# Joint attention tails, a rearranged start and held loads in a linear-attention plus feed-forward kernel

## The chip, the cores and the metric

One core of one Trainium2 chip. The metric is the device time in microseconds (us), median of several runs. A run of a program on few cores is called slow when it is over 1.5% above the fastest of the same kernel.

## The reference, cut to what matters

```python
def _attn_ref(q, k, v):              # batch 8, heads 8, sequence 576, head_dim 64
    phi = lambda x: np.where(x > 0, x, np.exp(x) - 1.0) + 1.0
    q_p, k_p = phi(q), phi(k)
    kv  = np.einsum('bhsd,bhse->bhde', k_p, v)
    z   = np.sum(k_p, axis=2)
    num = np.einsum('bhsd,bhde->bhse', q_p, kv)
    den = np.einsum('bhsd,bhd->bhs', q_p, z)[..., None] + 1e-06
    return num / den

def _moe_ref(x, w_in, w_out, beta):  # x: 4608 x 512, w_in: 512 x 2048, w_out: 2048 x 512
    h = x @ w_in
    g = h * (1.0 / (1.0 + np.exp(-beta * h)))
    return g @ w_out
```

## The kernel before

The program alternates, batch by batch, an h phase (`w_in` products and silu) and a y phase (`w_out` products and stores), 64 products of 512 columns each. The attention of the next batches is slipped in between. 576 rows are four tiles of 128 and a tail of 64; the tails of all eight batches form a ninth batch at the end. Each batch's tail was a pass of its own:

```python
    def num_mm(b, t):
        n = rows(t)                          # 128, or 64 for the tail
        nps = att_banks()
        st[b, "n", t] = nps
        for p in range(KC):                  # 4
            c0 = (p % 2) * 2 * (D + 1)
            nc.tensor.matmul(
                nps[:n, p // 2, c0 : c0 + 2 * (D + 1)],
                st[b, "qT"][:, t, p, :n],
                kv_bd[b % 2][p // 2][:, p % 2], ...)
    # num_norm: VectorE divides by the denominator, rows(t) rows.
    # x_trans: TensorE transposes x (batches 0-2); from batch 3 on the DMA does.
```

Batch 0 has a layout of its own (`nine`, nine columns of 64 rows), and the start loads it before the weights, all over the GpSimd queue:

```python
    load_nine(k9, k)
    load_nine(q9, q, j1=4)
    ...
    load_nine(v9, v, j1=6)
    load_nine(v9, v, j0=6)
    load_nine(q9, q, j0=4)
    for i in range(4):
        nc.gpsimd.dma_start(out=w_in_sb[i], in_=w_in_v[:, :, i * 512 : (i + 1) * 512])
    load_w_out(0); load_w_out(1); load_k(1); load_q(1)
    ...
    load_w_out(2); load_v(1); load_w_out(3)
```

Batch 4 is loaded in the second h phase, and q of batch 2 is transposed by DMA in the second y phase:

```python
            12: [F(v_copy, 2), F(load_next, 4)],          # second h phase
    ...
    y_phase_wide(1, {
        1: [F(phi, 2, 0), F(q_trans_dma, 2), F(phi, 2, 1)],
        6: [F(kv_mm, 2), F(kv_evac, 2)],
        11: [F(num_mm, 2, 0), F(num_norm, 2, 0)],
        12: [F(num_mm, 2, 1), F(num_norm, 2, 1), F(x_trans, 2, 0, wide=True)],
        ...
```

## Time and profile before

| what | before |
|---|---|
| time, median of 3 runs | 296.43 us (296.33 to 296.48) |
| TensorE busy | 283.9 of 295.1 us |
| first main product | 17.16 us |
| first h, first y phase | 17.00 and 18.37 us |
| second h, second y phase | 15.08 and 17.64 us |
| a steady batch (h and y) | 29.86 us |

The phases are read from the table of stretches, cut at the first product of each phase. Besides the lines that the prediction shows, two are needed for the comparison (start:end and length, busy us and number of instructions of TensorE, weight load, VectorE, ScalarE, GpSimd; granted TensorE clock, DMA share, GB/s):

```profile
34.16:52.53 18.37, 17.42 (x146) 9.32 (x148) 13.77 (x28) 13.69 (x15) 10.47 (x13) 1.00 1.42 248
...
85.42:101.36 15.94, 15.94 (x137) 9.20 (x136) 7.69 (x13) 12.65 (x23) 4.69 (x6) 1.00 0.94 138
```

The first, the first y phase, contains about 1 us of idle TensorE time, the second, batch 2's h phase, none. The second y phase is the stretch 67.61:85.25 of the prediction's table, with about 1.3 us idle.

### The profile page before, as it was taken

How to read it: one execution, taken by the hardware profiler on the slowest of the kernel's cores; microseconds unless marked ns; L12 is line 12 of the kernel's file. 1: busy time of each engine (PE TensorE's matmuls, PEld its weight loads, DVE VectorE, ACT ScalarE, POOL GpSimd, SP SyncE). 2: the span in 40 equal slices, each digit the busy share in tenths (PEclk: the TensorE clock that was granted, in tenths of full speed). 3: DMA queues.
4: the chain of work that ended last, by engine and by line, in shares of the span. 5: the costliest groups of instructions: out<-in, count | busy, mean ns of one | idle time of the engine just before them, and what ended most of it. 6: DMA issues, size and time to landing. Idle time of an engine off the chain costs nothing.

```text
span 295.1 us, 4750 instructions
## 1 busy us (share of the span) xinstructions
PE 283.9 (96%) x1891; PEld 143.9 (49%) x1912; DVE 124.0 (42%) x261; ACT 175.1 (59%) x234; POOL 52.7 (18%) x72
## 2 busy tenths in 40 slices
PE   8879999999999999999999999999999999999994
PEld 3557445644465544445444544454445444444444
DVE  4765488504365174616461646154715400110012
ACT  2788786889988780778087907790770077018500
POOL 8924474540003200330023000000000000000000
PEclk9999999999999999999999999999999999999999
DMA  7999999999637993699369945024502400120032
GB/s 103 196 207 343 256 272 192 256 193 192 89 142 100 175 131 113 130 174 154 98 129 159 159 109 124 2 71 116 127 0 72 118 36 0 38 90 16 0 73 71
DMA packets 72310, 37.09 MB, mean 126 GB/s; under 512 B 40912, under 2 KB 66784, under 8 KB 72288
## 3 DMA queue, kind: packets, MB, share of 16 engines
q0 software_dynamic: 38912, 20.45, 47.9%
q1 hardware_dynamic: 33216, 16.20, 22.9%
q8 instruction: 15, 0.25, 0.3%
q10 hardware_dynamic: 160, 0.13, 0.2%
q14 instruction: 7, 0.06, 0.1%
HBM read 36.71 MB, written 9.44 MB: 156 GB/s over the span
## 4 chain that ended last, share of the span: by engine, by line
PE 76%; DMA 9%; POOL 4%; ACT 4%; issue 4%; DVE 1%; ACTq 0%; POOLq 0%; DVEq 0%
PE mm L453 37%; PE mm L505 33%; DMA xT<-in_moe_w_out_dram 5%; DMA vraw<-in_v_dram 4%; PE att L399 3%; ACT e L229 2%; POOL xqk L131 1%; PE att L344 1%; PE mm L537 1%; POOL w_in L159 1%; ACT L229 1%; POOL vraw L131 1%; ACT g L445 1%; DVE qk_p L242 0%; POOL xqk L111 0%
## 5 line engine op out<-in xcount | busy, mean ns | idle before, releaser
L445 ACT ACTIVATE g<-mm,beta_c 128x512 bf16<-128x512 f32 (+2 forms) x156 | 97.3, 633 | 88.4 <-PE mm L453 88.1
L505 PE MATMUL mm<-w_out,g 128*128 128x512 bf16 x541 | 126.7, 379 | 1.2 <-issue 0.3
L453 PE MATMUL mm<-xT,w_in 128*128 128x512 bf16 (+2 forms) x560 | 108.1, 349 | 1.4 <-DMA w_in<-in_moe_w_in_dram 1.1
L453 PEld LDWEIGHTS <-w_in 128*128 128x128 bf16 x656 | 61.9, 98 | 62.4 <-DMA w_in<-in_moe_w_in_dram 1.2
L505 PEld LDWEIGHTS <-g 128*128 128x128 bf16 x560 | 53.0, 98 | 58.2
L515 DVE COPY y_sb<-mm 128x512 f32<-128x512 f32 x27 | 18.7, 691 | 70.6 <-PE mm L505 69.1
L229 ACT ACTIVATE e<-xqk 128x2560 bf16<-128x2560 bf16 x14 | 31.9, 2329 | 0.1
L415 DVE TENSOR_TENSOR xs<-att,rden 128x512 bf16<-128x512 f32 (+1 forms) x40 | 27.6, 689 | 1.4
L242 DVE TENSOR_TENSOR qk_p<-r,e 128x2560 bf16<-128x2560 bf16 x14 | 20.9, 1490 | 13.1 <-ACT e L229 12.4
L355 DVE CAST kv_bd<-att 64x130 bf16<-64x130 f32 x28 | 8.2, 292 | 32.2 <-PE att L344 31.8
L72 POOL DMA_DIRECT2D vraw<-in_v_dram x7 | 6.4, 909 | 84.2 <-DVE vaug L370 78.5
L413 DVE TENSOR_SCALAR den<-att 128x8 f32<-128x8 f32 (+1 forms) x40 | 6.5, 161 | 32.0 <-PE att L399 31.9
L399 PE MATMUL att<-kv_bd,q_pT 128*128 128x130 bf16 (+1 forms) x160 | 15.8, 221 | 1.1 <-DVE kv_bd L370 0.7
L399 PEld LDWEIGHTS <-q_pT 128*128 128x128 bf16 (+1 forms) x160 | 11.6, 100 | 10.7 <-DVE xs L415 2.4
L453 PE MATMUL mm<-xT_tail,w_in 128*128 128x512 bf16 x63 | 13.9, 379 | 0.1
L237 DVE TENSOR_SCALAR r<-xqk 128x2560 bf16<-128x2560 bf16 x14 | 11.6, 834 | 3.8 <-DMA xqk<-in_q_dram 2.3
L575 PE MATMUL mm<-g 128*128 128x512 bf16 x34 | 9.9, 452 | 1.2 <-DVE g L143 1.2
L229 ACT ACT_TABLE_LOAD x7 | 9.0, 1283 | 0.1
L414 DVE RECIPROCAL rden<-den 128x8 f32<-128x8 f32 (+1 forms) x40 | 8.1, 202 | 1.4
L72 POOL DMA_DIRECT2D xqk<-in_k_dram x7 | 6.9, 984 | 6.3 <-DMA w_in<-in_moe_w_in_dram 2.8
L76 POOL DMA_DIRECT2D xqk<-in_k_dram x7 | 7.4, 1057 | 1.5 <-DMA w_in<-in_moe_w_in_dram 1.3
L256 ACT ACTIVATE e<-xqk 128x1280 bf16<-128x1280 bf16 (+1 forms) x4 | 4.4, 1155 | 5.4 <-DMA xqk<-in_k_dram 5.3
(71 smaller groups left out, 140.0 us busy)
## 6 DMA issues: line engine op xcount, KB each, us to landing
out_dram<-y_sb SPq DMA_DIRECT2D x28, 256.0 KB, 2.3
xqk<-in_k_dram POOLq DMA_DIRECT2D x7, 512.0 KB, 10.7
xqk<-in_q_dram POOLq DMA_DIRECT2D x7, 512.0 KB, 11.3
vraw<-in_v_dram POOLq DMA_DIRECT2D x7, 512.0 KB, 11.3
w_in<-in_moe_w_in_dram POOLq DMA_DIRECT2D x4, 512.0 KB, 11.0
g<-in_moe_w_out_dram POOLq DMA_DIRECT2D x4, 512.0 KB, 10.9
out_dram<-y_sb SPq DMA_DIRECT2D x14, 128.0 KB, 5.2
xqk<-in_moe_w_out_dram POOLq DMA_DIRECT2D x2, 512.0 KB, 14.4
```

What stands on the lines that cost most here:

```text
L72: eng.dma_start(out=dst[:, :, 0:NJ, :].rearrange("p h j d -> p h (j d)"), in_=src[b, :, 0:MAIN, :].rearrange("h (p j) d -> p h (j d)", j=NJ),)
L229: nc.scalar.activation(st[b, "e", a][:, h0:h1], xqk[b % NX][:, a, h0:h1], ACTF.Exp)
L237: nc.vector.tensor_scalar(st[b, "r", a][:, h0:h1], xqk[b % NX][:, a, h0:h1], 0.0, 1.0, ALU.max, ALU.add)
L242: nc.vector.tensor_tensor(st[b, "p"][:, a].rearrange("p j (h d) -> p h j d", h=H)[:, h0:h1], st[b, "r", a][:, h0:h1], st[b, "e", a][:, h0: ...
L355: nc.vector.tensor_copy(kv_bd[b % 2][i][gs, :, g, :], st[b, "kvp"][gs, 2 * i : 2 * i + 2, :])
L399: nc.tensor.matmul(nps[:n, p // 2, c0 : c0 + 2 * (D + 1)], st[b, "qT"][:, t, p, :n], kv_bd[b % 2][p // 2][:, p % 2], start=True, stop=True ...
L415: nc.vector.tensor_mul(xs[:n], nv[:, :, :, 0:D], rden[:n, :, :, None].to_broadcast([n, 2, 4, D]))
L445: nc.scalar.activation(g_sb[b % 2][:, ff, c0:c1], hp[:, c0:c1], ACTF.Silu, scale=beta_c[:, ff : ff + 1],)
L453: nc.tensor.matmul(hp[:, c0:c1], w_in_sb[ff // 4][:, kc, (ff % 4) * P : (ff % 4 + 1) * P], x[:, t0:t1, kc, :] if b < B else x[:, kc, c0:c1 ...
L505: nc.tensor.matmul(yp, g_sb[b % 2][:, ff, t * P : (t + 1) * P], w_out_sb[ff // 4][:, ff % 4, :], start=(ff == 0), stop=(ff == FC - 1),)
L515: nc.vector.tensor_copy(y_sb, yp)
L575: nc.tensor.matmul(st["warm"], g_sb[0][:, FC - 1, 0:P], g_sb[0][:, FC - 1, :], start=True, stop=True, skip_group_check=True,)
```

## The change

Its intent: two neighbouring batches share one tail pass; batch 0's attention starts on a part of k; loads no longer run among DMA transposes that TensorE waits for. The core of the diff, cut:

```diff
+    load_nine(k_last, k, KF, N9, eng=nc.sync)       # KF = 5: k's last 4 columns, fp32
-    nc.sync.dma_start(out=beta_row, ...)
+    nc.scalar.dma_start(out=beta_row, ...)
-    load_nine(k9, k)
-    load_nine(q9, q, j1=4)
+    load_nine(x9[1][:, :, 0:KF], k, 0, KF)
+    load_nine(x9[0][:, :, 0:QF], q, 0, QF)          # QF = 4
-    load_nine(v9, v, j1=6)
-    load_nine(v9, v, j0=6)
+    load_nine(v9[:, :, 0:KF], v, 0, KF)
+    load_nine(v9[:, :, KF:N9], v, KF, N9)
 ...
-    warm(20)
+    warm(15)                                         # idle-time products
 ...                                                  # start and first h phase reordered
     def num_mm(b, t):
+            for i in range(1 if t < NJ else 2):
+                bb, n, r0 = (b, P, 0) if t < NJ else (b - 1 + i, TAIL, i * TAIL)
                 nc.tensor.matmul(
-                nps[:n, p // 2, c0 : c0 + 2 * (D + 1)], st[b, "qT"][:, t, p, :n], ...
+                    nps[r0 : r0 + n, p // 2, c0 : c0 + 2 * (D + 1)], st[bb, "qT"][:, t, p, :n], ...
     def num_norm(b, t):
-        if by_dma(b):
+        if by_dma(b) or t == NJ:                     # every tail transposed by DMA
 ...
+    def hold(a):
+        nc.gpsimd.tensor_copy(held, a)               # makes the GpSimd queue wait for a
+    def held_load(b, n):                             # batch b behind batch n's transposed q
+        hold(st[n, "qT"][0:1, NJ, KC - 1, 0:1])
+        load_next(b)
 ...
-        9: [F(kv_mm, 1), F(kv_evac, 1), F(w_out_scale, 3)],                # first y phase
-        10: [F(q_trans, 1, 0, 1, wide=True), F(q_trans, 1, 2, 3, wide=True)],
+        10: [F(q_trans, 1, 0, 1, 2, 3), F(kv_mm, 1), F(kv_evac, 1), F(w_out_scale, 3, 2)],
 ...
-            12: [F(v_copy, 2), F(load_next, 4)],
+            12: [F(v_copy, 2)],
-        6: [F(kv_mm, 2), F(kv_evac, 2)],
+        6: [F(kv_mm, 2), F(kv_evac, 2), F(held_load, 4, 2)],
-        12: [..., F(x_trans, 2, 0, wide=True)],
+        12: [..., F(x_trans, 2, 0, wide=True, dve=True)],   # x copies on VectorE
 ...
-        load_next(b + 3)
+            plan[7 + o] = [F(v_copy, n), F(held_v, b + 3, n)]
+            plan[12] = [F(held_kq, b + 3, n)]
-            for t in range(NT):
+            for t in range(NT if n % 2 else NJ):     # tail with every second batch
```

More of the change, by code (lines that the diff above doesn't have):

```diff
@@ L120, in nine, with load_nine @@
         flat = a.rearrange("p a b c -> p (a b c)")
-        size = {"h": HH, "j": N9, "d": D}
-        n = size["h"] * size["j"] * size["d"]
-        return flat[:, 0:n].rearrange(f"p ({names}) -> p {names}", **size)
-    q9 = nine(xqk[0][:, 0], "hjd")
-    k9 = nine(xqk[0][:, 1], "hjd")
-    v9 = nine(vraw[0], "hjd")
-    def load_nine(dst, src, h0=0, h1=HH, j0=0, j1=N9):
-        for g in range(2):
-            nc.gpsimd.dma_start(
-                out=dst[g * TAIL : (g + 1) * TAIL, h0:h1, j0:j1, :].rearrange(
-                    "p h j d -> p h (j d)"
-                ),
-                in_=src[0, g * HH + h0 : g * HH + h1, :, :]
+        return flat[:, 0 : HH * N9 * D].rearrange(
+            f"p ({names}) -> p {names}", h=HH, j=N9, d=D
+        )
+    x9 = [nine(xqk[0][:, a], "hjd") for a in range(2)]
+    v9 = nine(vraw[0], "hjd")
+    QF = 4
+    KF = 5
+    k_last = g_f[:, 0 : HH * (N9 - KF) * D].rearrange(
+        "p (h j d) -> p h j d", h=HH, j=N9 - KF
+    )
+    def load_nine(dst, src, j0, j1, eng=nc.gpsimd):
+        for g in range(2):
+            eng.dma_start(
+                out=dst[g * TAIL : (g + 1) * TAIL].rearrange("p h j d -> p h (j d)"),
+                in_=src[0, g * HH : (g + 1) * HH, :, :]
                 .rearrange("h (p j) d -> p h j d", j=N9)[:, :, j0:j1, :]
@@ L146 @@
     beta_row = consts.tile([FC, P], F32)
-    nc.sync.dma_start(out=beta_row, in_=moe_beta.rearrange("(c p) -> c p", p=P))
+    nc.scalar.dma_start(out=beta_row, in_=moe_beta.rearrange("(c p) -> c p", p=P))
     identity = consts.tile([P, P], BF16)
     ident16 = consts.tile([FC, FC], F32)
-    load_nine(k9, k)
-    load_nine(q9, q, j1=4)
+    load_nine(x9[1][:, :, 0:KF], k, 0, KF)
+    load_nine(x9[0][:, :, 0:QF], q, 0, QF)
     make_identity(nc, identity)
     make_identity(nc, ident16)
-    load_nine(v9, v, j1=6)
-    load_nine(v9, v, j0=6)
-    load_nine(q9, q, j0=4)
+    load_nine(v9[:, :, 0:KF], v, 0, KF)
+    load_nine(v9[:, :, KF:N9], v, KF, N9)
+    load_nine(x9[0][:, :, QF:N9], q, QF, N9)
     for i in range(4):
@@ L163 @@
     load_q(1)
-    kv_bd = [
-        [consts.tile([P, 2, 2, D + 1], BF16, name=f"kv_bd{i}{g}") for g in range(2)]
-        for i in range(2)
-    ]
+    kv_bd = [consts.tile([P, KC, 2, D + 1], BF16, name=f"kv_bd{i}") for i in range(2)]
     for i in range(2):
-        for g in range(2):
-            nc.vector.memset(kv_bd[i][g], 0.0)
+        nc.vector.memset(kv_bd[i], 0.0)
     def set_ones(i):
@@ L205, in make_beta, with w_out_scale @@
         nc.vector.reciprocal(rbeta, beta_c)
-    def w_out_scale(i, dve=True):
+    def w_out_scale(i, on_dve=4):
         for c in range(4):
@@ L210, in w_out_scale @@
             dst, src, by = w_out_sb[i][:, c, :], w_out_f[i][c // 2][:, c % 2, :], rbeta[:, ff : ff + 1]
-            if dve:
+            if c < on_dve:
                 nc.vector.tensor_scalar(dst, src, by, None, ALU.mult)
@@ L245, in phi, with begin9, in9, exp9 @@
         )
-    x0 = {0: q9, 1: k9}
+    def begin9():
+        begin(0)
+        st["p9"] = [
+            nine(st[0, "p"][:, a].rearrange("p j (h d) -> p j h d", h=H), "jhd")
+            for a in range(2)
+        ]
     def work9(tag, **kw):
         return nine(work.tile([P, H, NT, D], BF16, tag=tag, name=tag, **kw), "jhd")
-    def exp0(a, j0, j1):
+    def in9(a, j0, j1):
+        if a == 1 and j0 >= KF:
+            return k_last[:, :, j0 - KF : j1 - KF]
+        return x9[a][:, :, j0:j1]
+    def exp9(a, j0, j1):
         if j0 == 0:
-            st["e0", a] = work9("e", bufs=3)
+            st["e9", a] = work9("e", bufs=3)
         nc.scalar.activation(
-            st["e0", a][:, j0:j1].rearrange("p j h d -> p h j d"), x0[a][:, :, j0:j1],
+            st["e9", a][:, j0:j1].rearrange("p j h d -> p h j d"), in9(a, j0, j1),
             ACTF.Exp,
         )
-    def relu0(a, j0, j1):
+    def relu9(a, j0, j1):
         if j0 == 0:
-            st["r0", a] = work9("r")
+            st["r9", a] = work9("r")
         nc.vector.tensor_scalar(
-            st["r0", a][:, j0:j1].rearrange("p j h d -> p h j d"), x0[a][:, :, j0:j1],
+            st["r9", a][:, j0:j1].rearrange("p j h d -> p h j d"), in9(a, j0, j1),
             0.0, 1.0, ALU.max, ALU.add,
         )
-    def phi0(a, j0, j1):
+    def phi9(a, j0, j1):
         nc.vector.tensor_tensor(
-            st["p0"][a][:, j0:j1], st["r0", a][:, j0:j1], st["e0", a][:, j0:j1], ALU.min
+            st["p9"][a][:, j0:j1], st["r9", a][:, j0:j1], st["e9", a][:, j0:j1],
+            ALU.min,
         )
-    def q_trans0(t, banks, c0):
+    def q_trans9(t, banks, c0):
         for jj in range(2 if t < NJ else 1):
@@ L283, in q_trans0 @@
                         banks[:, g, m0 : m0 + TAIL],
-                        st["p0"][0][gs, 2 * t + jj, 2 * a : 2 * a + 2, :],
+                        st["p9"][0][gs, 2 * t + jj, 2 * a : 2 * a + 2, :],
                         identity[gs, gs],
@@ L287, in q_trans0, with q_out9 @@
                     )
-    def q_out0(t, banks, c0, dve):
-        n = rows(t)
-        src = banks[:, :, c0 : c0 + 2 * P].rearrange("p g (a n) -> p g a n", a=2)
-        dst = st[0, "qT"][:, t].rearrange("p (g a) n -> p g a n", g=2)
-        copy(dst[:, :, :, :n], src[:, :, :, :n], dve)
+    def q_out9(t0, t1, banks, c0, dve):
+        n = rows(t0)
+        src = banks[:, :, c0 : c0 + (t1 - t0) * 2 * P].rearrange(
+            "p g (t a n) -> p g t a n", a=2, n=P
+        )
+        dst = st[0, "qT"][:, t0:t1].rearrange("p t (g a) n -> p g t a n", g=2)
+        if n == P:
+            src = src.rearrange("p g t a n -> p g t (a n)")
+            dst = dst.rearrange("p g t a n -> p g t (a n)")
+        else:
+            src, dst = src[:, :, 0, :, :n], dst[:, :, 0, :, :n]
+        copy(dst, src, dve)
     def kv_cols(kvp, g, a):
@@ L308, in kv_mm0 @@
                         cols[:, :, 0:D] if of_v else cols[:, :, D],
-                        st["p0"][1][gs, j, 2 * a : 2 * a + 2, :],
+                        st["p9"][1][gs, j, 2 * a : 2 * a + 2, :],
                         v9[gs, 2 * a : 2 * a + 2, j, :] if of_v else ones[gs],
@@ L314, in kv_mm0, with kv_evac9 @@
                     )
-    def kv_evac0(kvp):
+    def kv_evac9(kvp):
         for g in range(2):
@@ L320, in kv_evac0 @@
                 copy(
-                    kv_bd[0][g][gs, :, i, :],
+                    kv_bd[0][gs, 2 * g : 2 * g + 2, i, :],
                     kvp[g][gs, 0 : 4 * (D + 1)].rearrange(
@@ L351, in kv_evac @@
     def kv_evac(b):
-        for i in range(2):
-            for g in range(2):
-                gs = slice(g * D, (g + 1) * D)
-                nc.vector.tensor_copy(
-                    kv_bd[b % 2][i][gs, :, g, :], st[b, "kvp"][gs, 2 * i : 2 * i + 2, :]
-                )
+        for g in range(2):
+            gs = slice(g * D, (g + 1) * D)
+            nc.vector.tensor_copy(kv_bd[b % 2][gs, :, g, :], st[b, "kvp"][gs])
     def rows(t):
@@ L372, in copy, with q_trans @@
             nc.scalar.activation(dst, src, ACTF.Copy)
-    def q_trans(b, *ts, wide=False, dve=False):
-        n, m = rows(ts[0]), len(ts)
-        tp = tr_bank(wide).rearrange("p (t c n) -> p t c n", t=2, c=KC)
+    def q_trans(b, *ts):
+        n = rows(ts[0])
+        tp = att_banks(BF16).rearrange("p i (t c n) -> p (i t) c n", t=2, c=KC)
         for i, t in enumerate(ts):
@@ L384, in q_trans @@
                 )
-        copy(st[b, "qT"][:, ts[0] : ts[0] + m, :, :n], tp[:, 0:m, :, :n], dve)
+        for i in range(0, len(ts), 2):
+            m = min(2, len(ts) - i)
+            copy(
+                st[b, "qT"][:, ts[i] : ts[i] + m, :, :n], tp[:, i : i + m, :, :n], False
+            )
     def q_trans_dma(b):
@@ L393, in num_mm @@
     def num_mm(b, t):
-        n = rows(t)
         nps = att_banks()
@@ L398, in num_mm @@
             c0 = (p % 2) * 2 * (D + 1)
-            nc.tensor.matmul(
-                nps[:n, p // 2, c0 : c0 + 2 * (D + 1)],
-                st[b, "qT"][:, t, p, :n],
-                kv_bd[b % 2][p // 2][:, p % 2],
-                start=True, stop=True, skip_group_check=True,
-            )
+            for i in range(1 if t < NJ else 2):
+                bb, n, r0 = (b, P, 0) if t < NJ else (b - 1 + i, TAIL, i * TAIL)
+                nc.tensor.matmul(
+                    nps[r0 : r0 + n, p // 2, c0 : c0 + 2 * (D + 1)],
+                    st[bb, "qT"][:, t, p, :n],
+                    kv_bd[bb % 2][:, p],
+                    start=True, stop=True, skip_group_check=True,
+                )
     def num_norm(b, t):
-        n = rows(t)
+        n = P
         den = work.tile([P, 2, 4], F32, tag="den", name="den")
@@ L425, in x_dst @@
             return xT[b % 3][:, t]
-        return xT_tail[:, :, b * TAIL : (b + 1) * TAIL]
+        return xT_tail[:, :, (b - 1) * TAIL : (b + 1) * TAIL]
     def x_trans(b, t, wide=False, dve=False):
-        n = rows(t)
+        n = P
         xv = st[b, "xs", t].rearrange("p a h d -> p (a h d)")
@@ L479, in h_last @@
             silu(b, 12 + i, hps[i])
-    out0 = out[0:S, :].rearrange("(p j) m -> p j m", j=N9)
+    out9 = out[0:S, :].rearrange("(p j) m -> p j m", j=N9)
     def tail_rows(b):
         if b == 0:
-            return out0[:, N9 - 1, :]
+            return out9[:, N9 - 1, :]
         return out[b * S + MAIN : (b + 1) * S, :]
@@ L492, in store @@
                     nc.sync.dma_start(
-                        out=out0[:, 2 * t + i, :], in_=y_sb[i * TAIL : (i + 1) * TAIL, :]
+                        out=out9[:, 2 * t + i, :], in_=y_sb[i * TAIL : (i + 1) * TAIL, :]
                     )
@@ L564, in load_next, with held_v, held_kq @@
         if b < B:
-            if b >= 5:
-                load_v(b)
             load_k(b)
             load_q(b)
-            if b < 5:
-                load_v(b)
+            load_v(b)
+    held = consts.tile([1, 1], BF16)
+    def hold(a):
[3 more added lines that the diff above has]
+        load_next(b)
+    def held_v(b, n):
+        if b < B:
+            hold(st[n, "qT"][0:1, NJ, KC - 1, 0:1])
+            load_v(b)
+    def held_kq(b, n):
+        if b < B:
+            hold(xT[n % 3][0:1, NJ - 1, KC - 1, 0:1])
+            load_k(b)
+            load_q(b)
     def warm(n):
@@ L584, in F @@
         return lambda: f(*a, **k)
-    begin(0)
+    begin9()
     st["warm"] = mm_bank([P, 512])
@@ L589 @@
     beta_trans()
-    make_beta()
-    warm(20)
-    st["p0"] = [
-        nine(st[0, "p"][:, a].rearrange("p j (h d) -> p j h d", h=H), "jhd")
-        for a in range(2)
-    ]
-    exp0(1, 0, 5)
-    exp0(1, 5, N9)
-    exp0(0, 0, 4)
-    relu0(1, 0, 5)
-    relu0(1, 5, N9)
-    phi0(1, 0, 5)
-    relu0(0, 0, 4)
-    phi0(1, 5, N9)
-    phi0(0, 0, 4)
+    warm(15)
+    exp9(1, 0, KF)
+    exp9(1, KF, N9)
+    exp9(0, 0, 2)
+    exp9(0, 2, QF)
+    relu9(1, 0, KF)
+    relu9(1, KF, N9)
+    phi9(1, 0, KF)
+    relu9(0, 0, QF)
+    phi9(1, KF, N9)
+    phi9(0, 0, 2)
+    phi9(0, 2, QF)
+    make_beta()
     kvp = [mm_bank([P, 512]) for _ in range(2)]
-    kv_mm0(kvp, 0, N9, False)
+    kv_mm0(kvp, 0, KF, False)
+    kv_mm0(kvp, 0, KF, True)
+    kv_mm0(kvp, KF, N9, False)
     qb = att_banks(BF16)
-    q_trans0(0, qb, 0)
-    q_trans0(1, qb, 256)
-    q_out0(0, qb, 0, False)
-    q_out0(1, qb, 256, False)
-    kv_mm0(kvp, 0, 6, True)
-    kv_mm0(kvp, 6, N9, True)
-    kv_evac0(kvp)
+    q_trans9(0, qb, 0)
+    q_out9(0, 1, qb, 0, False)
+    kv_mm0(kvp, KF, N9, True)
+    kv_evac9(kvp)
+    q_trans9(1, qb, 256)
+    q_out9(1, 2, qb, 256, False)
     st["warm"] = mm_bank([P, 512])
@@ L618 @@
     num_mm(0, 1)
-    exp0(0, 4, N9)
-    relu0(0, 4, N9)
+    num_norm(0, 0)
+    exp9(0, QF, N9)
+    relu9(0, QF, N9)
     silu_table()
-    num_norm(0, 0)
-    phi0(0, 4, 6)
     warm(4)
     x_trans(0, 0, dve=True)
+    num_norm(0, 1)
+    phi9(0, QF, 6)
+    phi9(0, 6, N9)
     qb2 = att_banks(BF16)
-    q_trans0(2, qb2, 0)
-    q_out0(2, qb2, 0, False)
-    num_norm(0, 1)
-    phi0(0, 6, N9)
     load_w_out(2)
@@ L635, with tidy, q_rest @@
     load_w_out(3)
-    def tidy0():
+    def tidy():
         clear_tail(0)
         nc.vector.memset(vraw[0][TAIL:P, :, NJ, :], 0.0)
-    def q_rest0():
-        q_trans0(3, qb2, 256)
-        q_trans0(4, qb2, 512)
-        q_out0(3, qb2, 256, False)
-        q_out0(4, qb2, 512, False)
+    def q_rest():
+        for t in range(2, NT):
+            q_trans9(t, qb2, (t - 2) * 256)
+        for t in range(2, NT):
+            q_out9(t, t + 1, qb2, (t - 2) * 256, t < NJ)
     h_phase(
@@ L652 @@
         {
-            3: [F(x_trans, 0, 1), F(num_mm, 0, 2), F(num_norm, 0, 2), F(q_rest0)],
-            5: [F(num_mm, 0, 3), F(num_norm, 0, 3)],
-            7: [F(x_trans, 0, 2)],
-            8: [F(num_mm, 0, 4), F(num_norm, 0, 4)],
-            9: [F(x_trans, 0, 3), F(tidy0)],
-            12: [F(x_trans, 0, 4)],
+            1: [F(x_trans, 0, 1)],
+            3: [F(q_rest)],
+            5: [F(num_mm, 0, 2), F(num_norm, 0, 2)],
+            7: [F(num_mm, 0, 3), F(num_norm, 0, 3)],
+            8: [F(x_trans, 0, 2)],
+            10: [F(x_trans, 0, 3, dve=True), F(tidy)],
             17: [F(w_out_scale, 0), F(w_out_scale, 1)],
@@ L674 @@
     phi(1, 1)
-    v_copy(1)
     phi(1, 0)
+    v_copy(1, 0, HH)
+    v_copy(1, HH, H, dve=False)
     y_phase_wide(0, {
         4: [F(load_next, 3)],
-        9: [F(kv_mm, 1), F(kv_evac, 1), F(w_out_scale, 3)],
-        10: [F(q_trans, 1, 0, 1, wide=True), F(q_trans, 1, 2, 3, wide=True)],
+        10: [
+            F(q_trans, 1, 0, 1, 2, 3), F(kv_mm, 1), F(kv_evac, 1), F(w_out_scale, 3, 2),
+        ],
         11: [F(num_mm, 1, 0), F(num_norm, 1, 0)],
@@ L683 @@
         13: [F(num_mm, 1, 2), F(num_norm, 1, 2), F(x_trans, 1, 1, wide=True)],
-        14: [F(num_mm, 1, 3), F(num_norm, 1, 3), F(q_trans, 1, 4, wide=True)],
+        14: [F(num_mm, 1, 3), F(num_norm, 1, 3), F(q_trans, 1, 4)],
     })
@@ L693 @@
             1: [F(x_trans, 1, 3)],
-            3: [F(x_trans, 1, 4)],
             8: [F(begin, 2), F(relu, 2, 0)],
             10: [F(relu, 2, 1)],
-            12: [F(v_copy, 2), F(load_next, 4)],
+            12: [F(v_copy, 2)],
         },
@@ L706 @@
         1: [F(phi, 2, 0), F(q_trans_dma, 2), F(phi, 2, 1)],
-        6: [F(kv_mm, 2), F(kv_evac, 2)],
+        6: [F(kv_mm, 2), F(kv_evac, 2), F(held_load, 4, 2)],
         11: [F(num_mm, 2, 0), F(num_norm, 2, 0)],
-        12: [F(num_mm, 2, 1), F(num_norm, 2, 1), F(x_trans, 2, 0, wide=True)],
-        13: [F(num_mm, 2, 2), F(num_norm, 2, 2), F(x_trans, 2, 1, wide=True)],
-        14: [F(num_mm, 2, 3), F(num_norm, 2, 3)],
+        12: [F(num_mm, 2, 1), F(num_norm, 2, 1), F(x_trans, 2, 0, wide=True, dve=True)],
+        13: [F(num_mm, 2, 2), F(num_norm, 2, 2)],
+        14: [
+            F(x_trans, 2, 1, wide=True, dve=True), F(num_mm, 2, 3), F(num_norm, 2, 3),
+        ],
     })
@@ L722 @@
             plan = {
-                0: [F(x_trans, 2, 2), F(num_mm, 2, 4), F(num_norm, 2, 4)],
-                1: [F(x_trans, 2, 3)],
-                3: [F(x_trans, 2, 4)],
+                0: [F(x_trans, 2, 2, dve=True)],
+                1: [F(x_trans, 2, 3, dve=True)],
             }
@@ L730 @@
             plan[5 + o] = [F(relu, n, 1), F(phi, n, 1)]
-            plan[7 + o] = [F(v_copy, n)]
+            plan[7 + o] = [F(v_copy, n), F(held_v, b + 3, n)]
             plan[12 + o] = [F(kv_mm, n)]
```

## The prediction

> **What bounds the kernel now.** I read the page first (busy shares and the 40 slices), then the chain of waits in order of time, then TensorE's timeline where that chain leaves TensorE, then the table of stretches, then the groups by shape.
>
> ```profile
> span 295.1 us, 4750 instructions
> ...
> PE 283.9 (96%) x1891; PEld 143.9 (49%) x1912; DVE 124.0 (42%) x261; ACT 175.1 (59%) x234; POOL 52.7 (18%) x72
> ...
> PE   8879999999999999999999999999999999999994
> ...
> DMA  7999999999637993699369945024502400120032
> ```
>
> TensorE is full in all slices but the first three and the last. The transfer engines are full too, up to about 80 us, and lightly used afterwards. So two regimes are to be expected: an early one in which arrivals matter, and a late one in which only TensorE's own work does. The chain in order of time (start, us, what) agrees:
>
> ```profile
> 13.18 15.45 DMA xT<-in_moe_w_out_dram
> ...
> 30.20 11.62 DMA vraw<-in_v_dram
> ...
> 110.91 0.35 PE att L399 x4
> 111.26 5.29 PE mm L505 x24
> 116.54 11.22 PE mm L453 x52
> 127.77 0.75 PE att L344 x40
> 128.52 2.70 PE mm L453 x12
> ```
>
> From about 83 us on the chain stays on TensorE. The 0.35 us is the tail of one batch: four products of 64 columns. The table of stretches (start:end, length, then busy time and count of TensorE, weight load, VectorE, ScalarE, GpSimd; clock, DMA share, GB/s), cut where the phases begin, says how much room each has:
>
> ```profile
> 17.16:34.16 17.00, 16.57 (x153) 11.31 (x154) 9.62 (x23) 13.87 (x32) 8.15 (x10) 1.00 1.29 263
> 34.16:47.30 13.14, 12.37 (x107) 6.46 (x108) 9.61 (x16) 10.39 (x9) 7.35 (x9) 1.00 1.36 272
> ...
> 67.61:85.25 17.64, 16.30 (x126) 8.14 (x128) 7.90 (x18) 16.99 (x17) 0.00 (x0) 1.00 0.89 135
> ...
> 128.52:158.38 29.86, 29.75 (x188) 14.25 (x190) 14.21 (x28) 18.12 (x20) 4.70 (x6) 1.00 0.83 137
> ```
>
> A steady batch has 0.11 us of idle time in 29.86: nothing is to be had there except by removing TensorE work. The room is in the early stretches, and the timeline of TensorE (start, us, instruction, in brackets the idle time before it and what ended it) names it:
>
> ```profile
> 17.16 1.07 PE L453 MATMUL mm<-xT,w_in 128*128 128x128 bf16 x16 [1.10 <-DMA w_in<-in_moe_w_in_dram]
> ...
> 19.28 0.61 PE L453 MATMUL mm<-xT,w_in 128*128 128x128 bf16 x8 [0.31 <-ACT xT L372]
> ...
> 43.23 0.82 PE L344 MATMUL att<-vaug,qk_p 128*64 128x65 bf16 x40 [0.28 <-DVE vaug L370]
> ...
> 79.33 0.41 PE L399 MATMUL att<-kv_bd,q_pT 128*128 128x130 bf16 x4 [0.34 <-DMA q_pT<-qk_p]
> ...
> 83.07 0.38 PE L433 MATMUL att<-identity,xs 128*128 128x128 bf16 x4 [0.61 <-ACT xT L372]
> ```
>
> The first main product waits for weights, not for the attention that feeds it. Busy time hides the shorter gaps, because ends are modelled; so I count work at the streaming rate: 52 products of 512 columns in 11.22 us are 0.216 us each, and a group of four full attention products is 0.22 to 0.23 us on the chain.
>
> [...] the 40 products of 64 by 65 above, alternating between output halves, take 0.75 us, 19 ns each, while the 64-column tail, all in one half, takes 0.35/4 = 87 ns each. [...] half of a v copy on ScalarE should bring no table load; here ScalarE's copies between silus have none.
>
> **Part by part.**
>
> Joint tails. Before, each batch has a tail pass of 0.35 us: 8 x 0.35 = 2.80. After, four passes of eight products that alternate between output halves. If the halves overlap, a pass costs about one old one, estimated 0.37: 1.48. Saved 1.32: batches 0 and 2 save 0.35 each early, the steady part (five passes become three) 5 x 0.35 - 3 x 0.37 = 0.64. The tails of batches 0, 1 and 2 no longer go through TensorE transposes (0.22 each on the chain), but by DMA: 0.66. Sum **1.98 us**, all on TensorE's path. VectorE loses four normalizations of about 1.05 us (0.16 + 0.20 + 0.68), off the path and worth nothing by themselves.
>
> Start. Four of nine columns of k now go over the sync queue, which can start at about 0.8 us where the first GpSimd transfer starts at 1.25. 0.52 MB of source thus moves mostly in engine time idle until 2.5 us, and everything behind in the GpSimd queue, w_in first, moves up by at most 0.52/0.4 = 1.3. The attention chain moves too: k's five columns land near 6.4 instead of 7.49, and xT would be ready near 14.5 instead of 16.3. w_in remains the later one, so I take its gain, less some interference: **1.0 us**, first main product at 16.1.
>
> First h phase (17.00 us). Work is 32 x 0.057 + 48 x 0.108 + 32 x 0.216 = 13.95, plus transposes of x 0.66 + 0.22, products 0.46 + 0.35, query transposes 0.35: 15.99, so 1.0 is idle. The new order puts eight more query transposes in (+0.23), but shifts consumers away from the ScalarE copy (0.31) and the short waits around it; the new VectorE copies make batch 0's third x late by some 0.2. I keep half of the idle time: net **0.27** beyond the tails.
>
> First y phase (13.14). Work to the second x tile is 48 x 0.216 + 0.75 + 0.87 + 0.23 = 12.2, idle 0.9. The kv product goes behind the query transposes and one more group, v's copy is split, two evacuations replace four. But the phase now starts 2 us sooner while w_out and v come only 1 us sooner; VectorE's two minimum passes, the evacuation and w_out's scaling end near 45.2 where TensorE wants the last weights near 45. I count half: **0.45**.
>
> Batch 2 (67.61 to 85.25). Work is 64 x 0.216 + 0.75 + 4 x 0.23 + 2 x 0.22 = 16.0, idle 1.65. Batch 4's loads no longer share the engines with batch 2's query transpose (9.0 us to landing in that window), which removes 0.27 to 0.34; the x copies go to VectorE and leave the queue behind ScalarE's exponentials, which removes 0.61 to 0.79. One wait of 0.3 for the first normalization stays, and VectorE has 4 x 1.06 + 4 x 0.42 = 5.9 us to do beside 5.2 of TensorE, so a little returns: **0.95**.
>
> Held loads from batch 5 on. These are off the path: there is no wait for q or x transposes in the steady part to remove. Expected 0.
>
> Sum: 1.98 + 1.0 + 0.27 + 0.45 + 0.95 = 4.65; 296.43 - 4.65 = **291.8 us**, 1.6% less.
>
> **Rivals.** (a) The second queue only shares: w_in is no earlier and the phases behind are paced by the same arrivals. For it: DMA is full at once from 2.5 us. Against: idle time before. It would cost about 1.3: 293.1. (b) The halves do not overlap, since each weight load of 64 columns waits: eight products at 87 ns are 0.70 and the joint pass saves nothing but the transposes; 293.1. Against: the kv products. (c) Held loads come too late: k and q are now issued some 3.5 us before the end of a y phase and wanted by the exponentials about 14.6 us after that end; at 11.3 us to landing they have near 7 us to spare. If they took 20 us, every batch would wait, and the gain would be gone: 296 or more. The lightly used engines speak against it. (d) The early phase is more elastic than I count: all of the idle time in the three early stretches goes and w_in moves 1.3. That adds 0.3 + 0.5 + 0.45 + 0.5: about 290.0.
>
> **Range and chances.** (a) and (b) are each perhaps one in six; (d) or a good part of it as likely. That gives 290.1 to 293.6. Faster by over 2% needs 290.5, 1.3 us beyond my sum: 0.16. Slower by over 2% needs (c) in force on several batches: 0.01. Within 2%: 0.83.
>
> **What would show it.** Right: the first main product near 16.1, still released by w_in; joint passes of eight in 0.3 to 0.45 us; no wait for q_pT and none for ScalarE's xT in the second y phase; steady batches of 29.5 and 29.9 us in turn; an end after the last product of 3.8 us as before. Wrong: a joint pass of 0.7; steady batches with a wait on k, q or v; an early phase waiting for w_out or on VectorE for over 1 us, which would mean that it was bound by arrivals more than I count.

For its figures: in the kernel before, the transfer engines moved 17 GB/s from 1.5 to 2.0 us, nothing from 2.0 to 2.5, 58 GB/s at a busy share of 0.77 from 2.5 to 3.0 ("full at once"), and 173 to 198 GB/s from 3.5 to 6.0 us, counted in bf16 as it is written; the prediction's 0.4 MB/us is an estimate, twice that for the fp32 source. The first exponential on k starts at 7.49 us. ScalarE's timeline has a table load of 1.28 us at 80.55 us and the next at 102.10, and none at the copies between the silus from 86 to 89 us; in the profile after, the half of the v copy on ScalarE, at 43.15 us, has none of its own. "Lightly used" holds for the late part of the row: its slices from 74 to 184 us read 3 to 9 tenths, those after them 0 to 5.

## The result, and the profile after

The changed kernel took 293.34 us (292.85 to 294.18, 4 runs), the kernel before 296.46 us beside it. The ratio is 0.9897 (95% interval 0.9873 to 0.9921): 1.0% faster. It lies inside the predicted range, 1.5 us above the predicted 291.8. Ratios here are the mean time of one kernel's fast runs over that of the other's of the same rounds, so not quite the ratio of the medians quoted.

The page's head and two of its rows of 40 slices:

```profile
span 292.3 us, 4708 instructions
...
PE 281.9 (96%) x1875; PEld 143.9 (49%) x1895; DVE 118.9 (41%) x239; ACT 173.7 (59%) x228; POOL 53.3 (18%) x79
...
PE   8779999999999999999999999999999999999994
...
PEclk9979999999999999999999999999999999999999
```

The third slice of the clock row is 7: TensorE's clock was lowered early in this run. All slices were 9 before. The stretches follow. From the second cut on they begin where the chain of waits enters a phase, 0.16 to 0.17 us after the first product of TensorE's timeline, where the table before was cut:

```profile
16.99:34.54 17.55, 17.47 (x153) 12.54 (x154) 9.36 (x22) 12.98 (x29) 8.20 (x10) 0.90 1.29 267
34.54:52.74 18.20, 17.66 (x149) 9.44 (x149) 12.18 (x24) 16.04 (x18) 11.08 (x13) 1.00 1.43 243
...
67.62:84.30 16.68, 16.15 (x127) 8.25 (x129) 8.46 (x18) 15.65 (x15) 4.87 (x7) 1.00 0.85 114
84.30:99.46 15.16, 15.16 (x129) 8.82 (x128) 7.20 (x10) 11.65 (x20) 1.74 (x3) 1.00 1.02 179
114.66:144.08 29.42, 29.32 (x184) 14.10 (x184) 13.03 (x23) 18.13 (x20) 7.59 (x11) 1.00 0.92 138
144.08:173.96 29.88, 29.77 (x192) 14.27 (x192) 13.93 (x26) 18.12 (x20) 3.55 (x7) 1.00 0.90 139
```

Read against the earlier tables: the first h phase is longer (17.40 by the timeline, 16.98 to 34.38, against 17.00), the first y phase almost unchanged (18.20 against 18.37). The second y phase is shorter by 0.96 us (16.68 against 17.64) and batch 2's h phase by 0.78 (15.16 against 15.94). Every second steady batch is shorter by 0.44 (29.42 against 29.86). The second y phase begins at 67.45 us by the timeline, where it began at 67.61 before; so in this run all but 0.16 of the 2.8 us in span came after that. The chain of waits shows the joint pass (start, us, what):

```profile
109.02 0.36 PE att L421 x8
109.38 5.29 PE mm L527 x24
```

Eight products take 0.36 us where four took 0.35: the halves overlap. In TensorE's timeline the first main product comes only 0.18 us sooner, batch 2's q is waited for no longer, and neither is ScalarE's copy of x:

```profile
16.98 0.62 PE L475 MATMUL mm<-xT,w_in 128*128 128x128 bf16 x8 [1.82 <-DVE qk_p L280]
...
78.67 0.40 PE L421 MATMUL att<-kv_bd,q_pT 128*128 128x130 bf16 x4
...
82.50 0.39 PE L455 MATMUL att<-identity,xs 128*128 128x128 bf16 x4
```

The first wait is put down to VectorE, but the weight load that belongs to it waited 2.0 us for w_in's DMA (table of waits: total us, times, longest):

```profile
PEld L475 <- DMA w_in<-in_moe_w_in_dram: 2.0, 1, 2.0
```

GpSimd, whose next load waits for the same transfer, went on at 17.22 us (17.41 before).

### The profile page after: what moved, and what is told of

Same layout as the page of the kernel before. It is cut to its first block, busy times and chain, and to the rows that moved or that the text cites. A ratio compares the mean times of both kernels' runs of the same rounds, so it can differ in the third digit from the quotient of the medians.

```text
span 292.3 us, 4708 instructions
## 1 busy us (share of the span) xinstructions
PE 281.9 (96%) x1875; PEld 143.9 (49%) x1895; DVE 118.9 (41%) x239; ACT 173.7 (59%) x228; POOL 53.3 (18%) x79
## 4 chain that ended last, share of the span: by engine, by line
PE 91%; DVE 3%; DMA 2%; ACT 1%; issue 1%; POOL 1%; ACTq 0%; POOLq 0%
PE mm L475 41%; PE mm L527 40%; PE att L421 3%; PE att L475 2%; DMA xqk<-in_q_dram 2%; PE att L362 2%; PE mm L559 1%; DVE xs L437 1%; ACT e L266 1%; PE mm L455 1%; ACT q_pT L387 1%; POOL xqk L135 1%; PE att L395 0%; DVE qk_p L280 0%; PE att L455 0%
## 5 line engine op out<-in xcount | busy, mean ns | idle before, releaser
L475 PEld LDWEIGHTS <-w_in 128*128 128x128 bf16 x656 | 63.0, 99 | 63.1 <-DMA w_in<-in_moe_w_in_dram 2.0
L242 DVE TENSOR_TENSOR qk_p<-r,e 128x2560 bf16<-128x2560 bf16 x14 | 20.9, 1491 | 13.1 <-ACT e L229 12.4
L437 DVE TENSOR_TENSOR xs<-att,rden 128x512 bf16<-128x512 f32 x36 | 24.9, 691 | 1.2
L372 DVE CAST kv_bd<-att 64x260 bf16<-64x260 f32 x14 | 6.0, 427 | 33.4 <-PE att L362 33.3
L435 DVE TENSOR_SCALAR den<-att 128x8 f32<-128x8 f32 x36 | 5.9, 163 | 30.1 <-PE att L421 30.0
L421 PE MATMUL att<-kv_bd,q_pT 128*128 128x130 bf16 (+1 forms) x160 | 14.7, 227 | 0.8 <-DVE kv_bd L385 0.4
L617 PE MATMUL mm<-g 128*128 128x512 bf16 x29 | 8.6, 449 | 1.3 <-DVE g L145 1.2
L72 POOL DMA_DIRECT2D xqk<-in_k_dram x7 | 6.8, 978 | 5.9 <-DMA w_in<-in_moe_w_in_dram 3.0
L436 DVE RECIPROCAL rden<-den 128x8 f32<-128x8 f32 x36 | 7.3, 203 | 1.2
L72 POOL DMA_DIRECT2D xqk<-in_q_dram x7 | 6.7, 963 | 3.8 <-DMA xqk<-in_k_dram 2.0
```

Of the source, the lines that this page charges most:

```text
L72: eng.dma_start(out=dst[:, :, 0:NJ, :].rearrange("p h j d -> p h (j d)"), in_=src[b, :, 0:MAIN, :].rearrange("h (p j) d -> p h (j d)", j=NJ),)
L242: nc.vector.tensor_tensor(st[b, "p"][:, a].rearrange("p j (h d) -> p h j d", h=H)[:, h0:h1], st[b, "r", a][:, h0:h1], st[b, "e", a][:, h0: ...
L421: nc.tensor.matmul(nps[r0 : r0 + n, p // 2, c0 : c0 + 2 * (D + 1)], st[bb, "qT"][:, t, p, :n], kv_bd[bb % 2][:, p], start=True, stop=True, ...
L436: nc.vector.reciprocal(rden[:n], den[:n])
L437: nc.vector.tensor_mul(xs[:n], nv[:, :, :, 0:D], rden[:n, :, :, None].to_broadcast([n, 2, 4, D]))
L475: nc.tensor.matmul(hp[:, c0:c1], w_in_sb[ff // 4][:, kc, (ff % 4) * P : (ff % 4 + 1) * P], x[:, t0:t1, kc, :] if b < B else x[:, kc, c0:c1 ...
```

## The experiments

Twelve runs, in three calls; kernels of one call shared a chip and the runs of the kernel before (medians 296.55, 296.79 and 297.08 us). The first two answer why the early part gained so little.

**The changed kernel again**

> The changed kernel once more, unedited, to see how often TensorE's clock falls in it. In its first profile the granted clock was 0.50 to 0.65 from about 18.3 to 21.7 us and the first h phase took 17.55 us (16.99 to 34.54 on the chain). Theory A (the changed start leaves TensorE idle enough for its clock to be halved in many runs): the mean granted clock is below 1.0 in more than half of the runs, and the runs that keep 1.0 are 0.5 to 1.0 us faster. Rival B (the first y phase is paced by arriving loads, so the lost clock is absorbed): times do not follow the clock; all lie within 0.4 us of one another.

Measured: 292.90 us (292.62 to 293.23), ratio 0.9886. In this trace the first main product came at 15.66 us, and the clock did not fall (mean 0.998). Over all eleven fast runs of the unedited changed kernel, four have a mean clock of 0.993 or 0.994 (mean time 293.71 us) and seven one of 0.997 to 1.000 (mean 292.97). In the traces a mean of 0.997 or more goes with no early dip. So the dip occurs in about a third of the runs, not in most, and goes with some 0.7 us; the runs are of several chips, so the size is rough. Neither theory holds as stated.

The dip is not the changed start's own, either. The run with the tails alone (below) has the old start, and its trace shows the same slowing: its first 16 main products, at 17.07 us, take 1.49 us where they take 1.07 in the kernel before, and the four transposes behind them 0.63 us where they take 0.39; and of the 21 runs of the kernel before, six have a mean of 0.991 to 0.993. What decides was not shown. Three of the 13 traces of fast runs have an early dip, after a wait for the first main product of 1.29 us (the tails alone), 1.82 us (the first profile) and 2.00 us (late loads not held); the other ten have none, after waits of 0.16 to 1.66 us. So in these traces the length of this wait alone does not separate them.

**More idle-time products**

```diff
-    warm(15)                       +    warm(20)
-    warm(1)                        +    warm(2)
     x_trans(0, 0, dve=True)
+    warm(7)
```

> The changed kernel with 13 more idle-time products at the start (20 instead of 15 before the attention, one more before the first numerators, 7 after the first x transpose, in the wait for the first weights). Theory A: the clock is 1.00 in every run and slice, the first h phase takes 15.9 to 16.2 us instead of 17.55, and the time falls by 0.7 to 1.2 us to about 292.3. Rival B (arrivals of batch 1's q and v and of the third and fourth part of w_out pace the first y phase): the first h phase is as much shorter, but the first y phase (18.2 us before) grows by as much, and the time is within 0.3 us of the changed kernel's.

Measured: 292.94 us (292.77 to 293.07), ratio 0.9883. The table of stretches, one us each, for the changed kernel's first profile (last but two column: granted clock) and for this one:

```profile
19.00:20.00 1.00, 1.00 (x12) 1.00 (x11) 0.67 (x2) 0.28 (x2) 0.69 (x1) 0.50 1.23 204
20.00:21.00 1.00, 1.00 (x12) 1.00 (x11) 0.62 (x3) 0.93 (x4) 0.00 (x0) 0.50 1.24 207
```

```profile
19.00:20.00 1.00, 1.00 (x17) 0.89 (x16) 0.76 (x4) 0.59 (x3) 0.69 (x1) 1.00 1.24 205
```

The clock stays full in the trace, and no run lies below 0.997; the first h phase takes 16.27 us instead of 17.40, the first y phase 18.20 in both, and the second h phase begins at 51.30 us instead of 52.58. So the time that a dip takes is not absorbed later: in this theory A was right, and not B, in which the first y phase would have grown. Yet the median does not move, since most runs have no dip to remove: in the second look above, without the added products, the second h phase began at 51.12. Rival B had the number right for another reason. Whether the products prevent every dip is not shown by four runs; the two edited kernels at the end of this section, without them, had none in four runs each either.

**k loaded whole**

```diff
-    load_nine(k_last, k, KF, N9, eng=nc.sync)
-    load_nine(x9[1][:, :, 0:KF], k, 0, KF)
+    load_nine(x9[1], k, 0, N9)
```

> The changed kernel with batch 0's k loaded whole over the GpSimd queue as before, and beta over the sync queue. My prediction's step (the sync queue uses idle transfer time and brings w_in 1.0 us forward): first main product about 0.8 to 1.0 us later than in the changed kernel, at 17.8, and the time 0.5 to 1.0 us longer. Theory that fell out of the first comparison (the two queues share the same engines, and the sync transfer's bytes start at about 2 us, with the others): first main product within 0.3 us of 16.98, time within 0.4 us.

Measured: 293.20 us (292.88 to 293.52), ratio 0.9892 against 0.9886 of the changed kernel on the same chip; the intervals overlap widely. The first main product came at 16.50 us, within the changed kernel's own spread. So a gain from the split of k over two queues is not measurable here (0.2 us by the ratios, 0.3 by the medians), and w_in comes as early without it. In this trace the second h phase began at 51.92 us, 0.8 later than in the second look, behind a wait of 0.78 us for q's minimum pass; one trace does not tell whether that is k's doing.

**The joint tails alone**

The kernel before with the new `num_mm`, `num_norm` and schedule of tails, and nothing else.

> The kernel before with nothing of the change but the joint tails (four passes of eight products instead of eight of four; the tails of batches 0, 1 and 2 transposed by DMA). My prediction's sum for this part is 1.98 us, so 294.5. If the part before the second h phase is paced by arriving loads, batch 0's 0.57 us is absorbed there and the rest stays: 1.2 to 1.5 us, so 295.0 to 295.3. If the halves do not overlap, a joint pass lasts 0.70 us and only some 0.7 us are gained.

Measured: 298.85 us (298.69 to 299.71), ratio 1.0089: 2.3 us slower, which none of the three expectations allowed. The chain of waits says where:

```profile
69.44 12.52 DMA q_pT<-qk_p
```

TensorE waited 3.9 us for batch 2's transposed q, and its clock was then 0.60 in the stretch from 82 to 84 us and 0.55 from 84 to 86. The transposes run among batch 4's loads, whose last packet came at 79.1 us instead of 75.3 before. That the additional tail transpose pushes those loads back, and that TensorE arrives 0.8 us sooner, fits; which weighs how much was not separated. A new theory follows (C): the hold is what lets the tails pay.

**Tails and hold of batch 4**

```diff
-            12: [F(v_copy, 2), F(load_next, 4)],
+            12: [F(v_copy, 2)],
-        6: [F(kv_mm, 2), F(kv_evac, 2)],
+        6: [F(kv_mm, 2), F(kv_evac, 2), F(held_load, 4, 2)],
```

> The kernel before with the joint tails and one thing more: batch 4's loads are held until batch 2's transposed q has landed. The tails alone lost 2.3 us, with a wait of 3.9 us for batch 2's q_pT, whose transposes took 12.5 us to landing among batch 4's loads (9.0 before, 4.9 in the changed kernel). Theory C (the tails by themselves push batch 4's loads later, into the transposes; the hold is what lets them pay): no wait for q_pT, landing near 5 us, time about 294.5 to 295.0, that is 4 us less than the tails alone. Rival D (the tails cost something else, such as the smaller weight loads or the longer clock dip): still 297 or more.

Measured: 295.19 us (294.83 to 295.55), ratio 0.9949. No wait for q_pT is left; batch 2's lands in 4.9 us. One line of TensorE's timeline names the next obstacle, the x copy behind ScalarE's exponentials:

```profile
82.33 0.38 PE L435 MATMUL att<-identity,xs 128*128 128x128 bf16 x4 [1.12 <-ACT xT L372]
```

**The late parts together**

The same, with batch 2's x copies on VectorE and the later loads held: everything but the new start, first h phase and first y phase.

> The kernel before with everything of the change after the first y phase and none of the new start: joint tails, batch 4 held, batch 2's x copies on VectorE, later loads held. What is then missing to the changed kernel is the worth of the new start, first h phase and first y phase. My prediction gave these 1.72 us beyond the tails, so it would be 294.6 where the changed kernel has 292.9. From the traces (second h phase begins 0 to 1.4 us earlier than before, of which batch 0's tail should be 0.5): 293.5 to 294.0.

Measured: 293.95 us (293.81 to 294.12), ratio 0.9908: 1.24 us less than tails and hold. The first two phases, still in the old order:

```profile
17.90:34.16 16.26, 15.84 (x145) 11.06 (x145) 7.76 (x20) 13.46 (x31) 7.64 (x10) 1.00 1.28 264
34.16:52.48 18.32, 17.43 (x146) 9.31 (x148) 14.27 (x29) 13.69 (x15) 11.13 (x13) 1.00 1.43 252
```

With batch 0's tail gone, the old order of the first h phase takes 16.26 us; the new order, at full clock, 16.27. The reordering of that phase by itself is worth nothing. Against the changed kernel's ratios (0.9897, 0.9886 and 0.9882 in three sets), the whole new start, first h and first y phase is worth 0.0011 to 0.0026, some 0.3 to 0.8 us.

**The changed kernel without the hold of batch 4**

> The changed kernel with batch 4's loads issued where they were before, unheld. Theory C: batch 2's transposes again take 9 to 13 us to landing, TensorE waits 2 to 4 us for them in the second y phase, and the time is 295 to 297. Predicted by my own sum for the hold alone (0.27 to 0.34 us): 293.2.

Measured: 297.95 us (296.79 to 298.73), ratio 1.0037: more than expected, and slower than the kernel before the change. TensorE's timeline, and the stretches after the wait (clock in the last column but two):

```profile
81.32 0.62 PE L421 MATMUL att<-kv_bd,q_pT 128*128 128x130 bf16 x4 [3.78 <-DMA q_pT<-qk_p]
81.73 1.92 PE L527 MATMUL mm<-w_out,g 128*128 128x512 bf16 x4
```

```profile
80.00:82.00 2.00, 0.68 (x5) 0.57 (x6) 0.02 (x1) 0.58 (x2) 0.00 (x0) 0.80 0.41 67
82.00:84.00 2.00, 2.00 (x10) 1.02 (x9) 1.04 (x3) 0.32 (x1) 0.00 (x0) 0.50 0.00 0
```

The wait costs twice: 3.78 us, and then the clock is halved, so four products take 1.92 us where they take 1.02 to 1.03 at full clock. Theory C stands.

**The hold alone**

The kernel before with only the two lines of the hold.

> The kernel before with the hold of batch 4's loads and nothing else (the tails stay single). My prediction's step: the hold removes the wait for batch 2's q_pT, 0.27 to 0.34 us, so 296.2 where before has 296.5. Rival from the traces: without it the next wait (a transposed x of batch 2 behind ScalarE's exponentials, 0.61 us before, 1.1 us in the run with tails and hold) takes its place, and the time is the same within 0.2. If the hold saved by itself what it saves beside the joint tails (about 3.7 us), it would be 293.

Measured: 296.98 us (296.40 to 297.57), ratio 1.0000 (0.9977 to 1.0022). Batch 2's q lands in 5.0 us instead of 9.0 and nobody waits for it, but the wait for ScalarE's x copy grew from 0.61 to 1.1 us in its place. The hold is worth nothing alone, and about 4 us beside the tails (1.0089 to 0.9949 in ratio, 298.85 to 295.19 us in median, on two chips).

**The later loads not held**

> The changed kernel with batches 5 to 7 loaded unheld after the h phase, v, k, q in that order, as before; batch 4 stays held. My prediction's step: the late holds are worth 0; time within 0.3 us of the control, steady batches of 29.4 and 29.9 us in turn. If they matter, as batch 4's hold does, TensorE waits for a q_pT or xT in the steady part and the time rises by more than 0.5 us.

Measured: 292.97 us (292.93 to 294.57), ratio 0.9879 against 0.9882 of the control: no difference beyond the noise, as predicted. The table of DMA issues (issuing queue, number, median us to landing) has a surprise, for the changed kernel and for this one:

```profile
q_pT<-qk_p SPq DMA_TRANSPOSE x6, 7.7
```

```profile
q_pT<-qk_p SPq DMA_TRANSPOSE x6, 4.8
```

The holds put the loads of k and q at the start of the next h phase, among the transposes of the next q, and lengthen them. It costs nothing because these are wanted only in the next y phase.

**The control**

> The changed kernel unedited, as a control on the same chip for the other three of this call: 292.9 to 293.4, ratio to the kernel before 0.9885 to 0.9900.

Measured: fast runs 293.19, 294.05 and 293.05 us, ratio 0.9882; the fourth, profiled, run was slow (304.28 us at a clock of 0.945) and is left out with its trace.

**Two attempts at the first y phase.** The first moved batch 1's second q copy to VectorE and split the scaling of w_out's third part around k's minimum pass.

```diff
-                copy(st[b, "qT"][...], tp[...], False)
+                copy(st[b, "qT"][...], tp[...], i > 0)
-    w_out_scale(2); phi(1, 1); phi(1, 0)
+    w_out_scale(2, 4, 0, 2); phi(1, 1); w_out_scale(2, 4, 2, 4); phi(1, 0)
```

> The changed kernel with two edits in the first y phase: the second of batch 1's two q copies goes to VectorE (idle there from 42.8 to 44.3 us while ScalarE does both, 1.94 us), and the second half of w_out's third part is scaled after k's minimum pass, so that q's minimum pass ends some 0.5 us earlier. If the first y phase waits on ScalarE and VectorE there: waits of 0.23, 0.30 and 0.34 us vanish and the time falls by 0.5 to 0.9. If it is paced by v's arrival at 41.4 us alone: within 0.2 of the changed kernel.

Measured: 293.42 us (293.08 to 293.87), ratio 0.9891: no gain. VectorE's copy waited for ScalarE's copy of the same tile, so the evacuation behind it came late, and TensorE waited for that:

```profile
44.70 0.69 DVE L385 COPY q_pT<-att 128x1024 bf16<-128x1024 bf16 x1 [1.99 <-ACT q_pT L387]
```

```profile
46.31 0.40 PE L421 MATMUL att<-kv_bd,q_pT 128*128 128x130 bf16 x4 [0.98 <-DVE kv_bd L372]
```

The second attempt kept the split, left both q copies on ScalarE, and filled VectorE's idle time with scaling:

```diff
     v_copy(1, HH, H, dve=False)
+    w_out_scale(3, 4, 0, 2)                  # before the evacuation, on VectorE
-            ..., F(kv_evac, 1), F(w_out_scale, 3, 2),
+            ..., F(kv_evac, 1), F(w_out_scale, 3, 3, 2, 4),   # 1 of 2 left on VectorE
```

> A second attempt at the first y phase: w_out's third part is scaled in two halves around k's minimum pass, and its fourth part's first half is scaled by VectorE before the kv evacuation, where it is idle for 1.5 us; a third quarter of it moves from ScalarE to VectorE. If the first y phase waits on these two engines: the waits of 0.23 and 0.34 us go and the first normalization starts earlier, 0.4 to 0.8 us less than the control. If v's arrival at 41.4 us and the copies behind it pace it: within 0.2 us of the control.

Measured: 292.37 us (292.07 to 292.85), ratio 0.9847 (0.9830 to 0.9864) against 0.9882 of the control. That is 0.8 us below the control's fast median of 293.19 and 1.0 below its mean of 293.43, one of whose three runs has the dip; without that run 0.7. So it is about what was expected, though the two intervals still touch. By the traces the second h phase begins at 50.59 us, and in the second look, whose first main product came at the same time, at 51.12. The group of four products behind the first numerator now takes 1.02 us instead of 1.36:

```profile
45.35 1.02 PE L527 MATMUL mm<-w_out,g 128*128 128x512 bf16 x4
```

Its result was correct, and it has the lowest time: 1.5% under the kernel before.

## Why the prediction was right or wrong

The range held by 0.3 us, near its upper end and close to the 293.1 us of rival (a). The sum was 4.65 us, the measured gain 3.1 us. That the terms came so near is in part luck, since two of them hung on each other in a way that the prediction did not see:

**Joint tails: size right, standing wrong.** A joint pass of eight products of 64 columns takes 0.36 us (0.37 estimated) where a pass of four took 0.35, so the halves overlap; odd batches run in 29.42, even ones in 29.88 us. A skipped pass even frees 0.44 us (29.86 to 29.42) rather than 0.35; why was not shown. But the prediction counted 1.98 us for the tails on their own, "all on TensorE's path". On their own they lost 2.3 us, as the run with the tails alone showed. Tails plus hold gained 1.60 us, where the prediction has 1.98 + 0.3.

**Batch 2: right in sum, wrong in its parts.** The second y phase became 0.96 us shorter (0.95 predicted). The prediction booked 0.27 to 0.34 us for the hold and 0.61 to 0.79 for the copies on VectorE. The hold alone is worth 0, since the next wait takes its place; the step from tails and hold to the late parts is 1.24 us, and since the late holds are worth 0, this is the copies'. Tails, hold and copies together: 2.84 us measured (296.79 to 293.95), 2.93 predicted. (The prediction's terms for this phase's work add up to 15.93 us, not 16.0; nothing hangs on it.)

**Start: the step that failed.** "w_in ... moves up by at most 0.52/0.4 = 1.3", taken as 1.0. In the profile after it was 0.18. The step took it that the second queue's 0.52 MB would move mostly in the engines' idle time before 2.5 us. In that profile the engines moved 41 GB/s from 2.0 to 2.5 us, about 0.02 MB, and next to nothing earlier; and the GpSimd queue's first packet came at 3.28 us, where it came at 2.70 before. By 7 us that queue had moved 0.47 MB, against 0.69 before: it was short by 0.22 MB, near the 0.26 MB (in bf16) that the split takes out of it, while the second queue moved 0.52 MB (in fp32). So the second queue took its time from the first, and the run with k whole agrees: the split brings no measurable time. Nor is an earlier w_in passed on. The second look and the changed kernel without the hold are the same program up to 51 us; their first main products came at 15.66 and 16.81 us, their second h phases began at 51.12 and 51.29. Of the 1.15 us, 0.17 arrived.

```profile
15.66 0.61 PE L475 MATMUL mm<-xT,w_in 128*128 128x128 bf16 x8 [0.52 <-DVE xT L385]
```

In the second look 0.43 us went to a wait for the normalization of x's second tile and 0.23 to one for q's minimum pass. VectorE's minimum passes for batch 1 begin at 39.48 us there, after it had waited for q until 35.98 us and for w_out's third part until 37.08 and 38.37 us. In the run with more idle-time products, whose first main product came at 16.83 us, they begin at 39.56, after waits until 35.82, 36.93 and 38.23 us: nearly the same times, whether w_in had come early or late. This is rival (a) of the prediction in both its halves: the second queue took from the first (0.47 against 0.69 MB by 7 us), and the phases behind are paced by the same arrivals. The attention chain missed its estimate too: x's first tile, for which the wait above is, was ready near 15.6 us and not near 14.5.

In seven fast traces with the changed start and the split, the first main product came at 15.66 to 17.17 us, mean 16.56; in the five with the old start at 16.97 to 17.90, mean 17.24. So about 0.7 us may be real, but it does not need the split; which part of the start it belongs to, and why the arrival varies by 1.5 us between traces, stays open.

**First h phase: 0.27 predicted, 0 found.** At full clock the old and the new order take the same time once the tail is gone. In some runs the clock falls in this phase, with the new start and with the old, which the prediction did not consider at all; it lengthened the phase by 1.1 us in the first profile (17.40 against 16.27). (The first three terms of the prediction's work add up to 13.92 us, not 13.95; nothing hangs on it.)

**First y phase: 0.45 predicted, 0.17 found in the first profile, none in the second (18.60).** As the prediction feared, VectorE and ScalarE have too much to do there: the second has waits of 0.23 us for k's and q's minimum passes, of 0.30 for a q copy, and a group of products stretched by 0.34. The second attempt removed the first and the last of these and recovered 0.7 to 1.0 us. So the phase was not paced by v's arrival alone.

Start, first h and first y phase together: 1.72 predicted beyond the tails, 0.3 to 0.8 measured. This is where most of the missing 1.5 us went. **Late holds: right at 0**, within the noise.

## What to carry to other kernels

A change can depend on another of the same diff: test each alone, and each removed, because shares from a sum do not show that one of them is what lets the other pay. A DMA transpose that an engine waits for should not be issued among bulk loads: batch 2's took 4.9 us to landing behind held loads, 9.0 us among loads in the kernel before, and 12.4 us in the changed kernel without the hold. Hold the loads until it has landed, as far as they have slack. A wait can cost again after it has ended: in that last run, behind a wait of 3.78 us, the clock was 0.50 from 82 to 84 us and four products took 1.92 us instead of 1.02 to 1.03. Count a second queue as worth nothing until a run shows otherwise (here 0.2 us by the ratios, within the noise), ask what arrives next behind a load that you bring forward, and when an engine is lightly used in a phase that waits, look at the order of its queue before moving work to it.
